# Clustered attention and a feed forward on one core: the first unit's transposed probabilities by halves in other banks, most weights made up later, the product with v by query tile, and other counts of places

## The chip, the cores and the metric

One core of one Trainium2 chip runs the kernel in one launch. The metric is the device time of an execution in microseconds (us). Before the change three runs gave a median of 846.21 us (845.62 to 848.19).

## The reference, cut to what matters

Attention over 4 batches, 8 heads, 768 positions and 64 columns a head, with a mask that lets a query see only the keys of its own cluster; the result, as 3072 tokens of 512 columns, goes through a feed forward of width 2048.

```python
def _attn_ref(q, k, v, centroids):
    ...
    q_assign = np.argmax(np.einsum('bhsd,hcd->bhsc', q_n, c_n), axis=-1)
    k_assign = np.argmax(np.einsum('bhsd,hcd->bhsc', k_n, c_n), axis=-1)
    mask = q_assign[:, :, :, None] == k_assign[:, :, None, :]
    scores = scale * np.matmul(q, k.transpose(0, 1, 3, 2))
    scores = np.where(mask, scores, -1000000000.0)
    scores = scores - np.max(scores, axis=-1, keepdims=True)
    attn = np.exp(scores)
    attn = attn / (np.sum(attn, axis=-1, keepdims=True) + 1e-09)
    return np.matmul(attn, v).astype(np.float32)

def _moe_ref(x, w_in, w_out):
    h = x @ w_in
    neg = h <= -1
    pos = h >= 1
    g = np.where(pos, h, np.where(neg, 0.0, (h + 1) ** 2 / 4))
    return (g @ w_out).astype(np.float32)
```

The weights arrive in float64; the kernel reads them as pairs of 32-bit words.

## The kernel before, in words

The work is cut into 12 units: a batch (4) and a third of its queries (256, in two query tiles t of 128). In a unit four head pairs hp follow each other, and in a pair four score tiles, one for each head j of the pair and query tile t. A score tile is 128 queries by 768 keys. TensorE writes it into a pair of banks (`pair`, two of them), VectorE adds the mask term and takes the row bound in one pass of 768 columns (`soften`, L1088, "score pass" below; it writes `sS`), and ScalarE takes the exponential with the row's sum (`at_soft`, L1104). The probabilities must then be transposed for the product with v.

In the first unit (`by_tensor`, L1138) all of this is in float32. TensorE transposes the tile in six matmuls of 128 columns into the same pair of banks that held the scores, and ScalarE copies 768 columns from there into `pT`. In all later units the tile is split into two float16 parts: ScalarE rounds it (`hl`), GpSimd subtracts the rounded part in two halves, and a DMA transpose issued on SP's queue brings both parts into `pT`. SP issues in its program's order.

The product with v (`at_av`, L1184) is a group of 72 matmuls of 64 columns for a head pair, both query tiles and both heads, in the first half of bank `banka`; VectorE scales it into `rb`, TensorE turns it back in the second half of that bank, and the result is `X[u]`, the feed forward's input.

The feed forward of a unit has eight columns f of 256. `ffn1` (L1347) multiplies X with `w_in` into one of three banks (`bankh`, `banki`, `bankj`, the ring `hid`); VectorE, ScalarE and VectorE again make the activation in `r`; ScalarE rounds it to `g`, GpSimd makes the remainder; `ffn2` multiplies with `w_out` into the second pair. The first unit's feed forward is float32 (`ffn1_first`, L1314), the later ones use float16 in two parts.

There are 16 blocks of weights, two for each f. A block is loaded in two halves (`w_load`, L1231), and `w_bits` (L1251) makes float32 from its word pairs: ScalarE takes the absolute value (1024 columns) into `wk`, VectorE shifts it (one TENSOR_SCALAR of 1024 columns) and combines twice (SCALAR_TENSOR_TENSOR of 1024 columns), and `w_sum` (L1279) has TensorE add columns up with a matrix of ones in 8 matmuls, of which VectorE takes a maximum (`w_am`). `w_split` (L1305) later makes the float16 parts.

The order is not written out by hand. Functions are filed under steps (`at`), the recorder notes every operation with a price and what it reads and writes, and a planner (`issue`, L363) sorts all engines' instructions by priorities: `BASE` passes forward and backward, then a table of numbers (`NUDGES`), each of which shifts the priorities of some functions. What is filed at a later step begins with a later priority. Buffers are rings (`new`, L546): the nth use of a ring of m places waits for the end of use n-m. The list `wat` holds the step of each block's `w_bits`. Before the change it runs from -4 by 2.2 a block. All recorded operations have the line L377 in the profile, so its rows are told apart by the names of their tiles.

Of the kernel before, what the change touches and what calls it, by code (L numbers as in the profile page):

```python
# [10 lines left out]
F16 = mybir.dt.float16  # L11
# [37 lines left out]
BASE = 3  # L49
NUDGES = (  # L50
# [422 lines left out]
class Ring:  # L473
# [4 lines left out]

    def __call__(self, *shape, dtype):
        self.i += 1  # L480
        return view(self.bufs[self.i % len(self.bufs)], shape, dtype)
# [16 lines left out]
def tile_clustered_attention_moe(  # L498
# [17 lines left out]
    P = 128  # L516
# [17 lines left out]
    WA, WR = -4, 2.2  # L534
# [34 lines left out]
    rings["x"] = Ring(tiles("x", 3, 4096) + wk[:1] + blocks[-1:] + [word[:, :1024], word[:, 1024:]])  # L569
# [17 lines left out]
    hid = Ring(one)  # L587
    start = cycle([0, 1]).__next__
# [96 lines left out]
    def batch_scale(b):  # L685

        e = BX[b]
        ar = misc(NP + 1)
# [82 lines left out]
    def k_first(hp):  # L771
# [12 lines left out]
        pn = misc(2, D)  # L784
# [60 lines left out]
    def k_scale(b, hp):  # L845
# [14 lines left out]
        ar = misc(1)  # L860
# [243 lines left out]
    def at_soft(b, hp, c, j, t):  # L1104
# [5 lines left out]
        if ("pT", j) not in e:  # L1110
            shape, kind = ([T, CT, P], F32) if by_tensor(b, c) else ([2 * T, CT, P], F16)
            e["pT", j] = new("pT", shape, kind, 3)
# [234 lines left out]
    def ffn1(u, f):  # L1347
        if u == 0:
            return ffn1_first(f)
        e = FS[u, f]  # L1350
        x = X[u]
        ph = hid(2, CQ, dtype=F32)
        for s in range(2):
# [204 lines left out]
```

## Time and profile before

| what | value |
|---|---|
| median of 3 runs | 846.21 us |
| the profiled execution | 844.95 us |
| its span, first to last instruction | 843.2 us |
| TensorE (PE) busy, with its granted clock over the span | 821.7 us, 0.992 |
| VectorE (DVE) busy | 633.7 us |
| ScalarE (ACT) busy | 645.7 us |
| GpSimd (POOL) busy | 481.3 us |
| DMA queue of SP, share of 16 rings' span | 83.2% |

The profile is of one execution. An engine's share is a mean over a start, in which keys, queries and weights are made ready and the first unit's attention runs, and a long stage, in which attention of later units and the feed forward of earlier ones share the engines; the rows by stretch tell the two apart. PE's busy time counts a matmul as long as it is modelled to be in the array, so a busy PE may still run at the lower clock, which the granted clock shows. DMA is the mean busy share of the 16 rings. A row of the timeline has its start, its length, and in brackets the idle time of its engine before it and what ended that.

### The profile page before, as it was taken

The numbers are of one execution on the slowest core, as the hardware profiler recorded it, in microseconds if no ns is written. First come the engines' busy times: TensorE is split into PE (matmuls) and PEld (weight loads), VectorE is DVE, ScalarE is ACT, GpSimd is POOL, SyncE is SP. The second block draws the span as 40 slices with busy tenths as digits, with TensorE's granted clock in tenths as the row PEclk, the third lists the DMA queues.
The fourth block names the chain that finished last, engine by engine and source line by source line (L and its number), as shares of the span: only waits on it lengthen the run. The fifth ranks groups of instructions, "written<-read, shape, count | busy, mean of one in ns | idle before, by whom it ended". The sixth has DMA issues, their size and how long they took to land.

```text
span 843.2 us, 21816 instructions
## 1 busy us (share of the span) xinstructions
PE 821.7 (97%) x8495; PEld 590.3 (70%) x8495; DVE 633.7 (75%) x1430; ACT 645.7 (77%) x1152; POOL 481.3 (57%) x541
## 2 busy tenths in 40 slices
PE   8887999999999999999999999999999999999998
PEld 6665667767666767776776777676676777777776
DVE  5899999989998787577897757678888767464322
ACT  5898978799977888888778788888787687675232
POOL 2012555466767768557667657667666577565122
PEclk9999999999999999999999999999999999999999
DMA  9866999989999989999999978999999887575000
GB/s 321 307 169 142 251 204 172 206 152 188 196 170 168 177 146 185 203 182 186 180 185 190 164 132 170 195 173 194 175 205 163 147 162 132 101 153 100 15 26 26
DMA packets 405415, 141.44 MB, mean 168 GB/s; under 512 B 373952, under 2 KB 397504, under 8 KB 405312
## 3 DMA queue, kind: packets, MB, share of 16 engines
q1 hardware_dynamic: 405312, 140.05, 83.2%
q8 instruction: 66, 1.08, 0.6%
q14 instruction: 37, 0.30, 0.1%
HBM read 40.40 MB, written 6.29 MB: 55 GB/s over the span
## 4 chain that ended last, share of the span: by engine, by line
PE 65%; DMA 2%; ACT 1%; issue 0%; DVE 0%; POOL 0%; ACTq 0%
PE pair L377 32%; PE banka L377 9%; PE banki L377 8%; PE bankh L377 8%; PE bankj L377 7%; DMA q<-qn 1%; DMA pT<-hl 1%; DMA kv<-n 1%; ACT sS L377 0%; POOL hl L377 0%; ACT hl L377 0%; ACT qn L377 0%; ACT q L377 0%; DVE sS L377 0%; DVE banki L377 0%
## 5 line engine op out<-in xcount | busy, mean ns | idle before, releaser
L377 POOL TENSOR_TENSOR hl<-sS,hl 128x384 f16<-128x384 f32 x352 | 334.5, 974 | 136.5 <-ACT hl L377 98.0
L377 PE MATMUL pair<-w,g 128*128 128x512 f16 (+2 forms) x1120 | 278.3, 387 | 0.0
L377 DVE CUSTOM_DVE_ANT_0 sS<-pair,zero,er 128x768 f32<-128x768 f32 x192 | 193.8, 1011 | 54.2 <-PE pair L377 36.1
L377 ACT ACTIVATE sS<-sS,sbi 128x768 f32<-128x768 f32 x192 | 179.0, 933 | 59.7 <-DVE sbi L377 52.3
L377 PEld LDWEIGHTS <-w 128*128 128x128 f16 x1848 | 179.2, 98 | 34.9 <-issue 1.5
L377 PEld LDWEIGHTS <-g 128*128 128x128 f16 x1104 | 105.9, 98 | 99.2
L377 PE MATMUL pair<-kv,q 128*128 128x384 f16 (+1 forms) x768 | 160.8, 345 | 2.1 <-ACT pT L377 0.7
L377 ACT CAST hl<-sS 128x768 f16<-128x768 f32 x176 | 144.2, 825 | 11.6 <-DMA pT<-hl 10.3
L377 POOL TENSOR_TENSOR g<-r,g 128x512 f16<-128x512 f32 x80 | 95.3, 1191 | 88.3 <-ACT g L377 79.4
L377 PEld LDWEIGHTS <-q 128*128 128x128 f16 x880 | 71.8, 98 | 45.3 <-issue 6.1
L377 PEld LDWEIGHTS <-pT 128*128 128x128 f16 x3168 | 98.3, 98 | 5.5 <-issue 1.1
L377 PE MATMUL banka<-kv,pT 128*128 128x64 f16 x3168 | 99.6, 193 | 0.0
L377 ACT ACTIVATE r<-r,f_ra,f_rs 128x512 f32<-128x512 f32 x80 | 64.8, 810 | 37.2 <-DVE r L377 36.8
L377 ACT CAST g<-r 128x512 f16<-128x512 f32 x80 | 48.8, 610 | 9.3 <-DVE r L377 6.4
L377 PE MATMUL bankj<-x,w 128*128 128x256 f16 (+1 forms) x368 | 47.9, 282 | 0.2 <-DVE r L377 0.2
L377 PE MATMUL bankh<-x,w 128*128 128x256 f16 (+1 forms) x320 | 42.0, 283 | 0.0
L377 PE MATMUL banki<-x,w 128*128 128x256 f16 (+1 forms) x280 | 41.5, 297 | 0.0
L377 POOL TENSOR_TENSOR qn<-qn,phi 128x256 f16<-128x256 f16 x44 | 26.7, 629 | 21.2 <-DVE bankj L377 5.3
L377 ACT ACTIVATION_READ_ACCUMULATOR sS<-sS,sbi 128x1 f32 x192 | 36.0, 187 | 0.0
L377 DVE TENSOR_SCALAR r<-bankh,f_lo,f_hi 128x512 f32<-128x512 f32 x27 | 21.8, 807 | 16.7 <-PE bankh L377 10.3
L377 DVE TENSOR_SCALAR r<-bankj,f_lo,f_hi 128x512 f32<-128x512 f32 x26 | 21.0, 806 | 16.6 <-PE bankj L377 10.5
L377 POOL CAST rr<-rs 128x4 f16<-128x4 f32 x4 | 2.8, 691 | 53.6 <-DVE bankh L377 29.2
(283 smaller groups left out, 1164.4 us busy)
## 6 DMA issues: line engine op xcount, KB each, us to landing
w<-in_moe_w_out_dram SPq DMA_DIRECT2D x14, 512.0 KB, 5.2
kv<-in_k_dram SPq DMA_DIRECT2D x16, 384.0 KB, 4.0
q<-in_q_dram SPq DMA_DIRECT2D x12, 512.0 KB, 4.8
kv<-in_v_dram SPq DMA_DIRECT2D x16, 384.0 KB, 5.1
out_dram<-o SPq DMA_DIRECT2D x11, 512.0 KB, 3.6
w<-in_moe_w_in_dram SPq DMA_DIRECT2D x10, 512.0 KB, 7.9
word<-in_moe_w_in_dram SPq DMA_DIRECT2D x6, 512.0 KB, 5.5
o<-in_v_dram SPq DMA_DIRECT2D x8, 384.0 KB, 3.9
```

The source lines that it names most:

```text
L377: fn(*args, **kw)
```

## The change

- In the first unit the transposes go, three at a time, into banks of the feed forward's ring `hid`, and each half of 384 columns is copied by itself. The pair of banks is no longer written by them.
- The step of the first 4 blocks' `w_bits` stays; those of the other 12 go to 14, 16, ... instead of 4.8, 7.0, .... The steps of the loads that reuse a place, of `w_scale` and `w_split` and of the first unit's feed forward follow from that list.
- Later units take their score tiles in the order of query tiles (both heads of t = 0, then of t = 1), `pT` is kept by query tile, and the product with v is two groups of 36 matmuls, one for each query tile. Product and turning back share one half of `banka`; the halves alternate (ring `av`).
- Small results (sums of weights, of squares, of ones) take a half of `banka` instead of a bank of `hid`.
- The ring of X has 3 places instead of 7. When the feed forward of unit 2 begins, the four places that were given up, with their sizes cut, extend the rings r, g, sS, hl and qn by one place each.
- `BASE` is 11 instead of 3, and the table of numbers is another one.

```diff
--- before.py
+++ after.py
@@ -46,38 +46,24 @@
 TURN, TURN_WAIT = dict(vector=185, gpsimd=118), 200
 
 LOOK, MARGIN = 0.4, 4000
-BASE = 3
+BASE = 11
 NUDGES = (
...
 )
 
 
@@ -476,6 +462,11 @@
     def __init__(self, bufs):
         self.bufs, self.i = bufs, -1
 
+    def extend(self, buf):
+
+        n = (self.i + 1) % len(self.bufs)
+        self.bufs, self.i = [buf] + self.bufs[n:] + self.bufs[:n], -1
+
     def __call__(self, *shape, dtype):
         self.i += 1
         return view(self.bufs[self.i % len(self.bufs)], shape, dtype)
@@ -531,7 +522,7 @@
     PRO = -14
     FA = SC + LA
     EARLY = 22
-    WA, WR = -4, 2.2
+    WA, WR, W2 = -4, 2.2, 14
     V_LATE, WG = 12.0, 2
 
     RAW = [3, 4, 5, 6, 7, 4, 5, 6, 0, 7, 6, 7, 0, 7, 0, 0]
@@ -566,7 +557,7 @@
     blocks = [wb[:, i * 1024 : (i + 1) * 1024] for i in range(2 * NF)]
     halves = wk[1:] + blocks[:-1]
     rings["w32"] = Ring(wk[:1])
-    rings["x"] = Ring(tiles("x", 3, 4096) + wk[:1] + blocks[-1:] + [word[:, :1024], word[:, 1024:]])
+    rings["x"] = Ring(tiles("x", 3, 4096))
     rings["g"] = Ring(tiles("g", 2, 2048))
 
     nb = tiles("n", 1, 2 * 3072)[0]
@@ -585,6 +576,7 @@
     pair = [psum.tile([P, 1024], F32, name=f"pair{i}") for i in range(2)]
     bank_a, *one = [psum.tile([P, 512], F32, name=f"bank{x}") for x in "ahij"]
     hid = Ring(one)
+    av = Ring([bank_a[:, :CQ], bank_a[:, CQ:]])
     start = cycle([0, 1]).__next__
 
     def early():
@@ -685,7 +677,7 @@
     def batch_scale(b):
 
         e = BX[b]
-        ar = misc(NP + 1)
+        ar = av(NP + 1, dtype=F32)
         am = e["am"].bitcast(BF16).rearrange("p (n a) -> p n a", a=2)[:, :, 1]
         rec.tensor.matmul(ar[:, :NP], ones, am, start=True, stop=True)
         mx = ar[:, NP:]
@@ -781,7 +773,7 @@
         )
         e["oneT"] = new("koT", [T * P], BF16)
         turned_ones(e["oneT"], one, T)
-        pn = misc(2, D)
+        pn = av(2, D, dtype=F32)
         with rec.group():
             for t in range(T):
                 rec.tensor.matmul(pn, ones, one[:, t], start=(t == 0), stop=(t == T - 1))
@@ -857,7 +849,7 @@
         rec.scalar.activation(out=junk, in_=e["k"].rearrange("p j f -> p (j f)"), func=AF.Square, accum_out=am)
 
 
-        ar = misc(1)
+        ar = av(1, dtype=F32)
         rec.tensor.matmul(ar, ones, am.bitcast(BF16)[:, 1:2], start=True, stop=True)
         sc = e["sc"] = new("sc", [1], F32, 2)
 
@@ -1107,24 +1099,26 @@
         sS, bi, pS = A.pop((b, hp, c, j, t))
         if "rs" not in e:
             e["rs"] = new("rs", [4], F32, 6)
-        if ("pT", j) not in e:
-            shape, kind = ([T, CT, P], F32) if by_tensor(b, c) else ([2 * T, CT, P], F16)
-            e["pT", j] = new("pT", shape, kind, 3)
+        m, w = (j, t) if by_tensor(b, c) else (t, j)
+        if ("pT", m) not in e:
+            shape, kind = ([T, CT, P], F32) if by_tensor(b, c) else ([2 * T, 2, P], F16)
+            e["pT", m] = new("pT", shape, kind, 3)
         sf = sS.rearrange("p a s -> p (a s)")
         rec.scalar.activation(
             out=sf, in_=sf, func=AF.Exp, bias=bi, scale=-1.0, accum_out=e["rs"][:, n : n + 1]
         )
-        pT = e["pT", j]
+        pT = e["pT", m]
         if by_tensor(b, c):
-            with rec.group():
-                for i in range(T):
-                    to = pS[:, i // 3, i % 3 * P : (i % 3 + 1) * P]
-                    rec.tensor.matmul(
-                        to, sf[:, i * P : (i + 1) * P], idf, start=(i % 3 == 0), stop=False, is_transpose=True,
-                        skip_group_check=True,
-                    )
-            pt = pS[:, :, :HS].rearrange("p h (n q) -> p h n q", q=P)
-            rec.scalar.copy(pT[:, :, t, :].rearrange("p (h n) q -> p h n q", h=2), pt)
+            for h in range(2):
+                ps = misc(T // 2, P)
+                with rec.group():
+                    for i in range(T // 2):
+                        x = (h * T // 2 + i) * P
+                        rec.tensor.matmul(
+                            ps[:, i], sf[:, x : x + P], idf, start=(i == 0), stop=(i == T // 2 - 1), is_transpose=True,
+                            skip_group_check=True,
+                        )
+                rec.scalar.copy(pT[:, h * T // 2 : (h + 1) * T // 2, t, :], ps)
             at_sums(e, n, b + c)
             return
         hl = new("hl", [2, S], F16, 3)
@@ -1132,7 +1126,7 @@
         for h in range(2):
             x = slice(h * HS, (h + 1) * HS)
             rec.gpsimd.tensor_tensor(out=hl[:, 1, x], in0=sf[:, x], in1=hl[:, 0, x], op=ALU.subtract)
-        rec.sync.dma_start_transpose(out=pT[:, :, t, :], in_=hl.rearrange("p a s -> p (a s)"))
+        rec.sync.dma_start_transpose(out=pT[:, :, w, :], in_=hl.rearrange("p a s -> p (a s)"))
         at_sums(e, n, b + c)
 
     def by_tensor(b, c):
@@ -1186,15 +1180,15 @@
         if u == 0:
             return at_av_first(hp)
         e, kv = A.pop((b, hp, c)), KV[b, hp]
-        pv, px = bank_a[:, :CQ], bank_a[:, CQ:]
-        with rec.group():
-            for t in range(CT):
+        pv = px = av(CQ, dtype=F32)
+        for t in range(CT):
+            with rec.group():
                 for j in range(2):
                     to = pv[:, (t * 2 + j) * D : (t * 2 + j + 1) * D]
                     for kc in range(T):
                         for i, (va, pa) in enumerate(((0, 0), (1, 0), (0, 1))):
                             rec.tensor.matmul(
-                                to, e["pT", j][:, pa * T + kc, t], kv["vs"][:, va, j, kc * D : (kc + 1) * D],
+                                to, e["pT", t][:, pa * T + kc, j], kv["vs"][:, va, j, kc * D : (kc + 1) * D],
                                 start=(kc == i == 0), stop=(kc == T - 1 and i == 2),
                             )
         xn = new("rb", [CT * 2, D], F32)
@@ -1282,7 +1276,7 @@
         n = 1024 if part is None else 512
         t = WL[a, f][:, (part or 0) * 512 :][:, :n]
         ab = t.bitcast(BF16).rearrange("p (f a) -> p f a", a=2)[:, :, 1]
-        pc = misc(P)
+        pc = av(P, dtype=F32)
         with rec.group():
             for x in range(n // P):
                 rec.tensor.matmul(pc, ones, ab[:, x * P : (x + 1) * P], start=(x == 0), stop=(x == n // P - 1))
@@ -1347,6 +1341,10 @@
     def ffn1(u, f):
         if u == 0:
             return ffn1_first(f)
+        if u == 2 and f == 0:
+            more = dict(r=wk[0][:, :512], g=wk[0][:, 512:], sS=word[:, :768], hl=word[:, 768:1536], qn=blocks[-1])
+            for name, buf in more.items():
+                rings[name].extend(buf)
         e = FS[u, f]
         x = X[u]
         ph = hid(2, CQ, dtype=F32)
@@ -1445,7 +1443,7 @@
     def at(step, fn, *args):
         ev.setdefault(step, []).append((fn, args))
 
-    wat = [WA + WR * i for i in range(2 * NF)]
+    wat = [WA + WR * i if i < 2 * WG else W2 + 2.0 * (i - 2 * WG) for i in range(2 * NF)]
     sf = 0
 
     def first(b, hp, c):
@@ -1485,7 +1483,7 @@
             for hp in range(NP):
                 s0 = first(b, hp, c)
                 for n in range(SC):
-                    j, t = divmod(n, CT) if u else (n % 2, n // 2)
+                    j, t = n % 2, n // 2
                     at(s0 + n, at_scores, b, hp, c, j, t)
                     at(s0 + n + 1, at_soft, b, hp, c, j, t)
                 at(s0 + (LA - 0.5 if u else LA - 1.5), at_av, b, hp, c)
```

On TensorE, the first unit, second query block of head pair 0 (`kv_62` holds head pair 1; `idf` is the identity). Before:

```order
L377 MATMUL pair_82<-idf,kv_64 64x128 x12
L377 MATMUL pair_83<-idf,sS_89 128x128 x6
L377 MATMUL bankj<-cf,kv_64 128x32 x6
L377 MATMUL pair_82<-idf,sS_88 128x128 x6
L377 LDWEIGHTS ones
L377 MATMUL banki<-wk_69,ones 128x128
...
L377 MATMUL pair_82<-kv_62,q_65 128x384
L377 MATMUL pair_83<-kv_62,q_65 128x384
L377 LDWEIGHTS hl_80
L377 MATMUL pair_82<-o_68,hl_80 128x384
```

After:

```order
L363 MATMUL bankj<-idf,sS_90 128x128 x3
L363 MATMUL pair_82<-kv_62,q_65 128x384
L363 MATMUL pair_83<-kv_62,q_65 128x384
L363 LDWEIGHTS hl_80
L363 MATMUL pair_82<-o_68,hl_80 128x384
...
L363 MATMUL bankj<-cf,kv_64 128x32 x6
L363 MATMUL banki<-idf,sS_88 128x128 x3
L363 LDWEIGHTS ones
L363 MATMUL banka<-wk_69,ones 128x128
...
L363 MATMUL banki<-idf,sS_89 128x128 x3
```

The transposes of a score tile stood between two uses of its pair of banks; now the next tile's scores are in the pair ahead of them, and the halves go into `banki`, `bankj` and `bankh`. The sum of a weights' block (`wk_69,ones`) has moved from `banki` to `banka`.

On VectorE, the first unit, from the 9th score pass (`ISA sS_88,sbi_135`) on; `wk_69` and `word_71` carry weights' words, `w_72` is the weights' memory. Before:

```order
L377 ISA sS_88,sbi_135<-pair_82,zero,er_132 128x768
L377 ISA sbi_135 128x1
L377 ISA sS_89,sbi_136<-pair_83,zero,er_132 128x768
L377 ISA sbi_136 128x1
L377 TENSOR_SCALAR wk_69<-wk_69 128x1024
L377 TENSOR_SCALAR banki<-banki 128x1
L377 SCALAR_TENSOR_TENSOR w_72<-w_72 128x1024
L377 TENSOR_SCALAR isx_165<-banki 128x1
L377 TENSOR_REDUCE w_am<-bankh 128x1
L377 TENSOR_REDUCE aq_160<-q_65 128x4
L377 SCALAR_TENSOR_TENSOR w_72<-w_72,wk_69 128x1024
L377 RECIPROCAL sv_168<-isx_165 128x1
```

After:

```order
L363 ISA sS_88,sbi_135<-pair_82,zero,er_132 128x768
L363 ISA sbi_135 128x1
L363 ISA sS_89,sbi_136<-pair_83,zero,er_132 128x768
L363 ISA sbi_136 128x1
L363 TENSOR_SCALAR banki<-banki 128x4
L363 TENSOR_SCALAR iq_161<-banki 128x4
L363 RECIPROCAL sq_163<-iq_161 128x4
L363 SCALAR_TENSOR_TENSOR n_78<-kv_61,sc_157,n_78 128x12x64
L363 SCALAR_TENSOR_TENSOR qn_67<-q_66,sq_163,qn_67 128x4x64 x4
L363 SCALAR_TENSOR_TENSOR w_72<-w_72 128x1024
L363 TENSOR_TENSOR x_73<-banka,rb_159 128x256
L363 SCALAR_TENSOR_TENSOR n_78<-kv_62,sc_158,n_78 128x12x64
```

Between the 9th pass and the 12 rows' end a shift, two combines and a maximum of weights (`wk_69`, `w_72`, `w_am`) stood in the queue; now one combine, and the remainders of k and q (`n_78`, `qn_67`) in their place.

## Rows read from the trace of the kernel before

**Rows 1.** Page, part 1: TensorE's busy time, share of the span, instructions.

```profile
PE 821.7 (97%) x8495; PEld 590.3 (70%) x8495; DVE 633.7 (75%) x1430; ACT 645.7 (77%) x1152; POOL 481.3 (57%) x541
```

**Rows 2.** Busy us by stretch: PE, PEld, DVE, ACT, POOL; clock, DMA share, GB/s.

```profile
24.00:83.56 59.56, 49.06 (x418) 36.43 (x419) 57.07 (x132) 54.22 (x95) 8.67 (x12) 0.91 0.71 198
83.56:190.65 107.09, 105.50 (x893) 73.95 (x893) 97.93 (x201) 90.56 (x160) 59.96 (x62) 0.98 0.96 197
190.65:262.18 71.53, 70.23 (x812) 49.91 (x811) 66.81 (x162) 61.17 (x106) 48.54 (x48) 1.00 0.99 178
85.51:839.32 753.81, 751.45 (x7853) 537.63 (x7853) 560.49 (x1257) 575.71 (x1037) 466.82 (x496) 1.00 0.85 160
```

**Rows 3.** Timeline of TensorE, two transposes of the first unit: start, length, [idle before].

```profile
68.22 2.27 PE L377 MATMUL pair<-idf,sS 128*128 128x128 f32 x12 [2.37 <-ACT sS L377]
...
85.51 2.31 PE L377 MATMUL pair<-idf,sS 128*128 128x128 f32 x12 [1.19 <-ACT sS L377]
```

**Rows 4.** Timeline of TensorE, the last matmuls.

```profile
838.50 0.82 PE L377 MATMUL banka<-w,g 128*128 128x256 f16 x6
```

**Rows 5.** Timeline of VectorE: the 11th, 16th and 60th score pass.

```profile
66.09 1.01 DVE L377 CUSTOM_DVE_ANT_0 sS<-pair,zero,er 128x768 f32<-128x768 f32 x1
...
83.56 1.01 DVE L377 CUSTOM_DVE_ANT_0 sS<-pair,zero,er 128x768 f32<-128x768 f32 x1
...
262.18 1.00 DVE L377 CUSTOM_DVE_ANT_0 sS<-pair,zero,er 128x768 f32<-128x768 f32 x1
```

**Rows 6.** Timeline of VectorE without a gap: a combine, two score passes, a maximum.

```profile
30.87 1.22 DVE L377 SCALAR_TENSOR_TENSOR w<-w,wk 128x1024 uint32<-128x1024 uint32 x1
32.00 1.01 DVE L377 CUSTOM_DVE_ANT_0 sS<-pair,zero,er 128x768 f32<-128x768 f32 x1
...
32.94 1.01 DVE L377 CUSTOM_DVE_ANT_0 sS<-pair,zero,er 128x768 f32<-128x768 f32 x1
...
35.11 0.28 DVE L377 TENSOR_REDUCE w_am<-bankj 128x1 f32<-128x128 f32 x1
```

**Rows 7.** VectorE by form, 24 to 96 us: busy us, mean ns | idle before.

```profile
L377 DVE SCALAR_TENSOR_TENSOR w<-w,wk 128x1024 uint32<-128x1024 uint32 x10 | 12.3, 1226 | 0.0
...
L377 DVE TENSOR_SCALAR wk<-wk 128x1024 uint32<-128x1024 uint32 x10 | 7.3, 731 | 0.4 <-ACT wk L377 0.4
```

**Rows 8.** Timeline of ScalarE in the first unit: copies, absolute value, 16th exponential's end.

```profile
44.58 0.35 ACT L377 COPY rb<-banka 128x256 f32<-128x256 f32 x1
...
46.21 1.15 ACT L377 ACTIVATE wk<-w 128x1024 f32<-128x1024 f32 x1
47.24 0.81 ACT L377 COPY pT<-pair 128x768 f32<-128x768 f32 x1
...
70.00 1.47 ACT L377 COPY pT<-pair 128x768 f32<-128x768 f32 x2
...
86.17 0.19 ACT L377 ACTIVATION_READ_ACCUMULATOR sS<-sS,sbi 128x1 f32 x1
```

**Rows 9.** VectorE by form, 96 to 160 us.

```profile
L377 DVE SCALAR_TENSOR_TENSOR w<-word 128x1024 uint32<-128x1024 uint32 x3 | 4.5, 1493 | 0.0
...
L377 DVE SCALAR_TENSOR_TENSOR w<-w 128x1024 uint32<-128x1024 uint32 x3 | 3.7, 1237 | 0.0
```

**Rows 10.** Busy time of a stretch of plain loads, and DMA issues of the page.

```profile
20.00:24.00 4.00, 2.86 (x36) 2.63 (x32) 3.90 (x13) 2.42 (x2) 0.00 (x0) 1.00 1.04 391
w<-in_moe_w_out_dram SPq DMA_DIRECT2D x14, 512.0 KB, 5.2
kv<-in_v_dram SPq DMA_DIRECT2D x16, 384.0 KB, 5.1
```

**Rows 11.** Timelines of VectorE and GpSimd: two long combines, and a subtraction beside them.

```profile
122.87 1.75 DVE L377 SCALAR_TENSOR_TENSOR word<-word,wk 128x1024 uint32<-128x1024 uint32 x1
...
124.88 1.84 DVE L377 SCALAR_TENSOR_TENSOR w<-word 128x1024 uint32<-128x1024 uint32 x1
...
124.72 2.77 POOL L377 TENSOR_TENSOR hl<-sS,hl 128x384 f16<-128x384 f32 x2 [1.18 <-ACT hl L377]
```

46 rows, old and new, of the table NUDGES are left out of this document.

## The prediction

> **What bounds the kernel now.** I read the page's engine shares first, then busy time by stretch, then the timeline of one engine at a time. The page gives TensorE 97% of the span [rows 1]; that is a mean over two stages. By stretch [rows 2] TensorE is busy 751.45 of the 753.81 us from 85.51 to 839.32, so from there on only 2.36 us can be won by any order. Before that the limit is VectorE: 57.07 of 59.56 us in the stretch from 24 to 83.56, in which the first unit's score passes lie, while TensorE works at a granted 0.91 and waits for ScalarE's exponentials (2.37 and 1.19 us [rows 3]). The last matmul ends at 839.32 [rows 4], and the output's way out takes the 3.9 us to the span's end. So the time is about 85.5 + 753.8 + 3.9 us inside the span: the change pays if TensorE becomes full earlier and then stays full. I count score passes (VectorE's 768-column pass over a pair of banks): the first unit's last is the 16th, at 83.56 [rows 5]; the 60th, at 262.18, is where the order has long made up all weights.
>
> **Term 1, VectorE up to the 16th pass.** Counted in the two instruction orders, the rows for weights that stand ahead of the 16th pass fall from 11 to 5 (shift, 1024 columns), from 19 to 10 (combine) and from 9 to 4 (maximum). A row ends about 0.08 us after the next can start (30.87 to 32.00 for a row of 1.22; 0.94 from pass to pass [rows 6]), so a shift costs 0.65, a combine 1.15 [rows 7], a maximum 0.20 [rows 6]. That takes away 6 x 0.65 + 9 x 1.15 + 5 x 0.20 = 15.2 us. One remainder of k and one of a weight now stand ahead instead, about 1.05 each: +2.1. Net 13 us: by VectorE alone the 16th pass could come at 70.5.
>
> **Term 2, ScalarE up to there.** Absolute values of weights ahead of the 16th exponential fall from 11 to 6, at 1.03 from start to start (46.21 to 47.24 [rows 8]): -5.2. The copies of turned probabilities go from 14 of 768 columns to 26 of 384. A copy of 768 takes 0.80, one of 256 takes 0.35 [rows 8]; one of 384 lies between them, on the line at 0.46, of which 0.1 overlaps the next. So 26 x 0.37 = 9.6 against 14 x 0.70 = 9.8: nothing (if 384 cost as much as 768, +8.4). Smaller rows moved behind: -1.2. ScalarE's 16th exponential ended at 86.36 [rows 8], 2.8 after its pass began, and would end 6.6 earlier: the pass at 77.0. But ScalarE is idle 5.3 of the 59.56 us [rows 2], since a pair of banks is held from its score pass (66.09 [rows 5]) through exponential and transposes (68.22 [rows 3]) until the copies of 70.00 are through [rows 8], 5.4 us. With the halves in other banks a pair is free after the pass itself. Without that idle time the pass comes at 71.6. I take 75, between 71.6 and 77: **8.5 us gained** so far.
>
> **Term 3, what was put off comes back.** From the 16th to the 60th pass three resources need nearly the whole stretch of 178.62 us. VectorE is busy 97.93 + 66.81 = 164.74 [rows 2]. To that come back the 13 us, and a surcharge: ahead of 96 us, with GpSimd nearly idle, a combine takes 1.22; from 96 to 160 it takes 1.24 to 1.49 [rows 7, 9], about 0.18 more, for nine of them 1.6 us. Three remainders of q, some 0.5 each, now stand behind the 60th: -1.5. That is 177.8. TensorE is busy 105.50 + 70.23 = 175.7, and gets about 5 us more (five blocks' sums and part of a column of the feed forward; by order, priced row by row): 180.7. The DMA rings are busy 0.96 and 0.99 of it, 173.6; in SP's order six half loads of weights (512 KB) and two of v (384 KB) that stood ahead of the first DMA transpose of probabilities now stand among the first 44, 3.8 MB at the 391 GB/s of a stretch of plain loads [rows 10] or 9.8 us, less one transpose of about 2: 181.4. Each load also stands ahead of transposes on SP, which issues in order, and TensorE's products wait for those. With the 16th pass at 75 the three alone would put the 60th at 252.8, 255.7 and 256.4. They cannot all run without a gap: VectorE left 4% idle even where it was the limit [rows 2]. I take 184 us, 1.5% above the largest: 259.0, **3.2 us earlier** than 262.18. The ends are 180.7 and 188 (4% above).
>
> **Term 4, the rest.** Behind the 60th pass the work is the same. The product with v is split by query tile: in the order 36 of 44 products now stand as two runs of 36 matmuls with other work between, 8 stay whole; the number of matmuls is the same, so the split costs nothing while TensorE is full. The second place for r, qn and the extra ones for g, sS and hl can win only what TensorE idles, 2.36 us; I take 0.5, between 0 and 2.4. X falls from 7 places to 3: in the new order the feed forward of unit 0 is through near the 38th pass, and X's fourth user writes near the 52nd, so nothing waits there. The small sums moved from the feed forward's banks into the product's bank cost the same.
>
> Sum: 3.2 + 0.5 = 3.7 us. The profiled execution took 844.95 us (span 843.2 and 1.75 around it), 1.26 under the median of 846.21. So 846.2 - 3.7 = **842.5 us**. A measurement of this kernel tells 0.3%, 2.5 us, from no change: under 843.7 is faster, over 848.7 slower.
>
> **Rivals.** *All given back.* If the stretch to the 60th pass takes 187 us, the lead of 8.5 is gone, and only term 4 is left: 845.7. For it: three full resources in one stretch, with the added loads among the transposes. Against it: before, VectorE had 13.9 us idle there, which the postponed rows can fill. Under this also falls that the halves don't free ScalarE (pass at 77) or that the new places are never needed.
>
> *Everything meshes.* The 16th pass at 71.6, the stretch in 180.7, and all of term 4: 9.9 + 2.3, about 834. For it: VectorE ran without a gap for 50 us in the old order. Against it: TensorE would have to be full from the 16th pass on.
>
> *Slower, by GpSimd.* Now 22 combines instead of 13 stand behind the 16th pass, where GpSimd subtracts the rounded probabilities all the time. Two such rows took 1.75 and 1.84 us when they met a subtraction, and the subtraction itself was longer [rows 11]. If all 22 paid 0.40 more on the path, 8.8 us are added: 851. From 0.28 each on the kernel is slower by the bound above (6.2 us over 22). Against it: other combines in the same stretch take 1.24 [rows 9]. The Trainium skill (SBUF — State Buffer, section SBUF: two separate sides) says that VectorE with two SBUF inputs and a GpSimd operation that reads SBUF exclude each other for the whole instruction. By that rule, the long rows agree: an estimate with half of a subtraction lost on each would be 853.
>
> **Chances and range.** Forecast 0.40, everything meshes 0.14, all given back 0.32, slower 0.14. So faster 0.54, same 0.32, slower 0.14. The range goes from 835 (nearly all of the meshing case; ends 71.6 and 180.7) to 849.5 (the stretch at 188 with the pass at 77 gives 848.5, and part of the GpSimd case).
>
> **What would show it.** Right: the 16th pass near 75 instead of 83.56, the 60th near 259, TensorE's last wait of over a microsecond before 80, and a later stretch that is as full as before. Term 2 is wrong if the pass stays past 77 with ScalarE idle; term 3 if VectorE, SP or the transposes open gaps on TensorE between 90 and 260; the GpSimd case shows as combines of 1.6 us and more. Outside the range the forecast fails by a gap in the long stretch, which I hold for full.

## The result, and the profile after

The changed kernel takes a median of 837.42 us (836.36 to 839.2, four runs) against 847.2 us (845.62 to 848.56, four runs) for the kernel before beside it: ratio 0.989, 95% interval 0.9865 to 0.9915, so 9.8 us or 1.1% faster. The profiled executions took 836.59 us (span 834.8) and 844.95 us (span 843.2); the 8.4 us between these two are what the traces can explain.

Page of the changed kernel, part 1, against [rows 1]:

```profile
PE 819.3 (98%) x8495; PEld 586.2 (70%) x8495; DVE 631.6 (76%) x1430; ACT 646.8 (77%) x1168; POOL 485.1 (58%) x541
```

TensorE idles 834.8 - 819.3 = 15.5 us of the span instead of 21.5, and is busy 2.4 us less with the same 8495 matmuls. Busy time by stretch of the changed kernel (columns as in [rows 2]), cut at its own 16th, 44th and 60th score pass, then the long full stretch:

```profile
24.00:72.14 48.14, 43.41 (x379) 28.98 (x378) 46.86 (x120) 46.84 (x98) 5.36 (x12) 1.00 0.77 213
72.14:185.60 113.46, 108.86 (x964) 76.47 (x962) 111.03 (x220) 95.51 (x169) 66.12 (x61) 1.00 0.95 198
185.60:255.19 69.59, 69.12 (x788) 49.44 (x786) 68.53 (x160) 61.84 (x107) 50.50 (x49) 1.00 0.90 177
72.14:255.19 183.05, 177.98 (x1750) 125.91 (x1748) 179.56 (x379) 157.35 (x275) 116.62 (x109) 1.00 0.93 190
85.06:830.90 745.84, 743.32 (x7819) 533.02 (x7817) 559.23 (x1251) 572.32 (x1026) 467.00 (x489) 1.00 0.85 163
```

Timeline of VectorE, the 16th and 60th pass, against 83.56 and 262.18 in [rows 5]:

```profile
72.14 1.01 DVE L363 CUSTOM_DVE_ANT_0 sS<-pair,zero,er 128x768 f32<-128x768 f32 x1
...
255.19 1.01 DVE L363 CUSTOM_DVE_ANT_0 word<-pair,zero,er 128x768 f32<-128x768 f32 x1
```

Timeline of TensorE, its waits of over a microsecond after the 16th pass, and the last matmuls, against [rows 3, 4]:

```profile
73.77 0.55 PE L363 MATMUL bankj<-idf,sS 128*128 128x128 f32 x3 [1.41 <-ACT sS L363]
...
83.84 0.81 PE L363 MATMUL pair<-kv,q 128*128 128x384 f16 x4 [1.22 <-DVE sbi L363]
...
830.14 0.82 PE L363 MATMUL banka<-w,g 128*128 128x256 f16 x6
```

The 16th pass comes 11.4 us earlier, the 60th 7.0. TensorE accounts for all of the 8.4 us. Its idle time by stretch, before and after:

| stretch | before | after |
|---|---|---|
| up to 24 us | 3.45 | 1.55 |
| from there to the 16th pass | 10.50 | 4.73 |
| 16th to 60th pass | 2.90 | 5.07 |
| 60th pass to the end | 4.67 | 4.20 |

That is 6.0 us less; the 2.4 us less of busy time (granted clock 1.00 from 24 on, against 0.91 up to the 16th pass) are the rest. From 8 to 24 us TensorE has no idle time any more; these 1.9 us stand in no term of the prediction. The last wait of over a microsecond ends at 83.84 instead of 85.51 (from 83.84 to 85.06 there is no gap), and by then TensorE has done 819.26 - 743.32 - 1.22 = 74.7 us of work instead of 821.67 - 751.45 = 70.2. From 85.06 to the last matmul it idles 2.52 us, against 2.36 from 85.51 [rows 2].

### The profile page after: what moved, and what is told of

Its sections match the earlier page's. It is cut to its first block, busy times and chain, and to the rows that moved or that the text cites. A ratio compares the mean times of both kernels' runs of the same rounds, so it can differ in the third digit from the quotient of the medians.

```text
span 834.8 us, 21762 instructions
## 1 busy us (share of the span) xinstructions
PE 819.3 (98%) x8495; PEld 586.2 (70%) x8495; DVE 631.6 (76%) x1430; ACT 646.8 (77%) x1168; POOL 485.1 (58%) x541
## 4 chain that ended last, share of the span: by engine, by line
PE 76%; DVE 14%; DMA 4%; issue 3%; ACT 2%; POOL 1%; SPq 0%; DVEq 0%; POOLq 0%
PE pair L363 37%; PE banka L363 11%; PE banki L363 10%; PE bankh L363 9%; PE bankj L363 9%; DVE sS L363 4%; DVE w L363 3%; DMA q<-in_q_dram 1%; DMA w<-in_moe_w_out_dram 1%; DVE r L363 1%; DVE n L363 1%; DVE wk L363 1%; POOL hl L363 1%; DMA pT<-hl 1%; DMA kv<-n 1%
## 5 line engine op out<-in xcount | busy, mean ns | idle before, releaser
L363 POOL TENSOR_TENSOR hl<-sS,hl 128x384 f16<-128x384 f32 x212 | 210.0, 1011 | 96.1 <-ACT hl L363 70.1
L363 PE MATMUL pair<-w,g 128*128 128x512 f16 (+2 forms) x796 | 202.6, 393 | 0.0
L363 PEld LDWEIGHTS <-q 128*128 128x128 f16 x880 | 71.6, 97 | 48.3 <-issue 8.0
L363 ACT CAST hl<-sS 128x768 f16<-128x768 f32 x106 | 87.4, 825 | 1.7 <-DMA pT<-hl 0.7
L363 PE MATMUL banki<-x,w 128*128 128x256 f16 (+1 forms) x672 | 86.0, 280 | 0.0
L363 PE MATMUL bankh<-x,w 128*128 128x256 f16 (+1 forms) x672 | 85.8, 280 | 0.1
L363 PEld LDWEIGHTS <-wk 128*128 128x128 f16 x606 | 58.0, 98 | 34.8 <-issue 0.6
L363 POOL TENSOR_TENSOR hl<-word,hl 128x384 f16<-128x384 f32 x70 | 63.1, 921 | 31.3 <-ACT hl L363 20.4
L363 POOL TENSOR_TENSOR word<-sS,word 128x384 f16<-128x384 f32 x70 | 64.0, 932 | 24.8 <-ACT word L363 22.6
L363 PE MATMUL pair<-w,wk 128*128 128x512 f16 x324 | 76.3, 373 | 0.0
L363 POOL TENSOR_TENSOR g<-r,g 128x512 f16<-128x512 f32 x32 | 39.8, 1244 | 26.1 <-ACT g L363 26.1
```

Of the source, the lines that this page charges most:

```text
L363: fn(*args, **kw)
```

## The experiments

Theory A: the parts of the code bring the gain, the place for the halves first. B: the newly found order brings it, that is the table and the 11 passes. C: the later weights bring it alone. In nine runs the table of numbers is empty and the order planned anew, since a table found for one code says nothing for another. The first two keep the planner's number of passes of their kernel, 11 and 3; for the other seven it was chosen anew, among 3 to 16. These nine (times are medians; the 16th and 60th score pass are those of one profiled execution):

| kernel, no table | time | ratio to before, interval | 16th pass | 16th to 60th |
|---|---|---|---|---|
| all parts | 840.66 | 0.9924, 0.9898 to 0.9949 | 73.25 | 186.45 |
| no part | 855.72 | 1.0107, 1.0072 to 1.0141 | 84.46 | 184.18 |
| without halves | 850.37 | 1.0039, 1.0018 to 1.0060 | 82.56 | 182.06 |
| without late weights | 848.67 | 1.0037, 1.0012 to 1.0063 | 78.92 | 184.31 |
| small results in the ring | 850.93 | 1.0049, 1.0031 to 1.0068 | 72.10 | 189.45 |
| product whole | 845.55 | 0.9983, 0.9971 to 0.9994 | 70.17 | 196.45 |
| without new places | 843.55 | 0.9966, 0.9953 to 0.9980 | 72.78 | 193.30 |
| halves alone | 851.57 | 1.0065, 1.0039 to 1.0091 | 79.71 | 186.26 |
| late weights alone | 858.74 | 1.0141, 1.0099 to 1.0183 | 83.06 | 190.24 |

**Code or order.** The table is taken out of the changed kernel, and out of the kernel before.

```diff
-NUDGES = (1525064232, ...)
+NUDGES = ()
```

> The changed kernel with the table of numbers taken out (no priorities shifted by it), BASE 11 kept: the code's parts remain, the found order goes. Theory A (the parts of the code bring the gain: places for the halves first, the later weights second): most of the gain stays; the table is worth 3 to 5 us to the changed kernel as it is to the kernel before, so about 841, still some 8 under the kernel before without its table. Theory B (the new table and BASE bring the gain, the parts are about neutral): 845 to 849, level with the kernel before without its table.

> The kernel before with its table taken out, BASE 3 kept. Both theories expect it slower than with the table, by 3 to 5 us: 849 to 852. Theory A wants it some 8 us above the changed kernel without its table, theory B level with it (within 2.5 us).

Without tables the parts gain 855.7 - 840.7 = 15.1 us, so the new table does not bring the gain. The number of planner's passes, B's other half, still differs here, 11 against 3. Against it speak the runs below: with a number of their own, undoing one main part costs 8.0 or 9.7 us, and one part alone put into the kernel before, with 11 or 16 of them, gains 4.1 us or nothing. The table is worth 3.2 us to the changed kernel, as expected, and 8.7 to the kernel before (847.0 beside it), more than expected: it may already have made up for part of what the code lacked there.

In the two profiles (spans 838.9 and 852.4) TensorE idles 20.9 and 26.6 us and is busy 818.0 and 825.8, with the same 8495 matmuls, at a mean granted clock of 0.995 and 0.989. So more than half of the difference lies in its busy time; how much of that is the clock's, these two do not tell.

**Halves undone.**

```diff
-for h in range(2):
-    ps = misc(T // 2, P)
...
+for i in range(T):
+    to = pS[:, i // 3, i % 3 * P : (i % 3 + 1) * P]
...
+rec.scalar.copy(pT[:, :, t, :].rearrange("p (h n) q -> p h n q", h=2), pt)
```

> The changed kernel without a table, and the first unit's transposes again all six in the pair of banks with one copy of 768 columns; the planner orders it anew (8 passes, the best of 3 to 16 by its own measure; 11 for the changed kernel). Theory A: the pair is held through exponential, transposes and copy again, ScalarE idles again about 5 us before the 16th score pass, the pass comes 4 us later or more, TensorE's clock falls again; 845 to 851, that is 4 to 10 above the changed kernel without its table. Theory B: within 2.5 us of it. A third theory, C (the later weights bring the gain, by VectorE alone): within 2.5 us of it, 16th pass near 72.

Busy time by stretch, up to the 16th pass: all parts, then without halves.

```profile
24.00:73.25 49.25, 40.93 (x365) 27.47 (x361) 46.37 (x115) 45.75 (x96) 7.06 (x12) 0.97 0.75 208
```

```profile
24.00:82.56 58.56, 47.07 (x387) 32.62 (x387) 51.26 (x129) 53.67 (x99) 7.72 (x13) 0.94 0.72 193
```

The pass comes 9.3 us later and the time rises by 9.7. ScalarE idles 4.9 us of the stretch instead of 3.5, and VectorE, which has its weights put off, 7.3 instead of 2.9: neither is full. The time is theory A's, and C falls. The date of the pass overstates the waiting: ScalarE is also busy 7.9 us longer ahead of it, mostly with rows that make keys and queries ready, and TensorE idles only 4.0 us more up to the pass.

**Late weights undone.**

```diff
-wat = [WA + WR * i if i < 2 * WG else W2 + 2.0 * (i - 2 * WG) for i in range(2 * NF)]
+wat = [WA + WR * i for i in range(2 * NF)]
```

> The changed kernel without a table, and the weights' bits asked for at the old steps (2.2 apart from -4 on); ordered anew (6 passes). Theory A: 13 us of VectorE stand ahead of the 16th pass again, so the pass comes at 80 or later; part of that is made up behind it since less weight work is left there: 2 to 6 us above the changed kernel without its table. Theory B: within 2.5 us. Theory C: all the gain goes, 8 us or more above.

The time rises by 8.0 us, more than theory A allowed and about C's least, though of a gain of 15.1. The pass comes at 78.92, 5.7 us later, and the stretch to the 60th gets 2.1 us shorter: so much of the lead is given back when weights are put off. At the 60th pass 3.5 us are lost, of 6.7 between the two profiled executions. TensorE idles 26.4 us of the span instead of 20.9, and 3.9 of these 5.5 lie between the two passes: weights asked for early cost most behind the 16th pass, which theory A did not expect. Why is open.

**One part alone.** The two main parts, each put by itself into the kernel before.

> The kernel before (no table, ordered anew, 11 passes) with one part of the change: the first unit's transposes by halves in the feed forward's banks. The kernel before without its table took 855.7 us with its 16th pass at 84.46; VectorE was busy 58.52 of the 60.46 us from 24 on. Theory A (parts that need each other): VectorE still has all its weights ahead, so the pass comes only 2 us earlier, and the time falls by 2 to 5 us, to 851 to 854. Rival (halves are the whole gain): 16th pass near 74, time near 841 to 844.

> The kernel before (no table, ordered anew, 16 passes) with one part of the change: the later steps for the bits of 12 blocks of weights. Theory A: VectorE is unloaded, but the pair of banks is held as before, so the 16th pass comes at 80 to 83 and the weights stand behind it: no gain, 853 to 857. Rival (late weights bring a gain by themselves): 16th pass at 77 or earlier, 848 or less.

Busy time by stretch, up to the 16th pass: halves alone, then late weights alone.

```profile
24.00:79.71 55.71, 46.34 (x431) 31.80 (x431) 54.97 (x131) 52.41 (x107) 5.32 (x12) 0.97 0.69 197
```

```profile
24.00:83.06 59.06, 45.56 (x414) 31.75 (x414) 55.43 (x133) 53.41 (x93) 7.47 (x13) 1.00 0.71 187
```

With the halves alone VectorE is busy 54.97 of 55.71 us: it is the bound. The pass comes 4.8 us earlier, more than theory A's 2, and 4.1 us are gained (the intervals overlap a little). With the late weights alone nothing is gained, and the pass moves by 1.4 us. For the date of the pass the parts need each other: alone they move it by 4.8 and 1.4 us, both together by 12.4, in the next run. For the time they are not enough: that run has both, with the split product and the new places, and lacks only the move of the small results; it is 4.8 us under no part, not 15.1.

**Small results back in the ring.** These stand in the prediction as free.

```diff
-pc = av(P, dtype=F32)
+pc = misc(P)
```

The four other `av(...)` of small results go back in the same way.

> The changed kernel (no table, 840.7 us; ordered anew, 5 passes) with its small results (sums of weights, squares and ones) back in the three banks of the feed forward. The prediction held this part for free. Theory A (only the halves and the later weights count): within 2.5 us of 840.7, 16th pass near 73. Rival (the ring of three banks must be kept for the halves): each sum takes a turn of the ring, TensorE or ScalarE waits for a bank, 16th pass 3 us later or more and 845 or more.

Waits of TensorE from 73 to 265 us (total, times, longest): this run, then all parts without a table.

```profile
PE pair L346 <- DVE sbi L346: 2.3, 5, 0.9
PE bankh L346 <- DVE w_am L346: 1.8, 2, 1.0
PE banki L346 <- DVE w L346: 1.5, 2, 1.2
PE bankh L346 <- DVE r L346: 1.3, 1, 1.3
PE banki L346 <- DVE banki L346: 1.0, 1, 1.0
PE banki L346 <- DVE r L346: 0.9, 3, 0.5
PE bankj L346 <- DVE g L346: 0.9, 1, 0.9
```

```profile
PE pair L346 <- DVE sbi L346: 2.0, 3, 1.3
PE banka L346 <- DVE wk L346: 1.0, 1, 1.0
PE banki L346 <- ACT pT L346: 0.9, 1, 0.9
```

As costly to undo as the halves: 10.3 us, with the 16th pass as early as ever, so the rival has the time right and not the place. From the 16th to the 60th pass TensorE idles 12.2 us instead of 5.5. In the rows shown it waits 7.4 us for VectorE at the banks h, i and j, 9.1 with the smaller ones; the other kernel's list has 0.2 of that. Two of these waits, 1.8 us, are for the maximum (`w_am`) itself: a sum holds one of three banks until VectorE has taken it. That the others follow from the same is argued, not shown: VectorE has 184.39 us of work in those 189.45, and whoever takes the next bank stands behind it, but it is as full with all parts (182.35 of 186.45).

**Product whole, and places undone.**

```diff
-pv = px = av(CQ, dtype=F32)
-for t in range(CT):
-    with rec.group():
+pv, px = bank_a[:, :CQ], bank_a[:, CQ:]
+with rec.group():
+    for t in range(CT):
```

```diff
-rings["x"] = Ring(tiles("x", 3, 4096))
+rings["x"] = Ring(tiles("x", 3, 4096) + wk[:1] + blocks[-1:] + [word[:, :1024], word[:, 1024:]])
...
-        rings[name].extend(buf)
```

> The changed kernel (no table, 840.7 us; ordered anew, 16 passes) with the product with v as before: score tiles by heads, one group of 72 matmuls, product and turning back in the two halves of the bank. Theory A: the split is worth 0 to 2.5 us, all of it behind the 16th pass (TensorE's idle time from there to the 60th grows from 5.5 us); 840 to 843. Rival (the split is what keeps TensorE fed while the weights come back): the 16th pass as early, but the stretch to the 60th 4 us longer or more, 845 or more.

> The changed kernel without a table, ordered anew (11 passes), with seven places for X and none lent to r, g, sS, hl and qn. Without a table the changed kernel took 840.7 us; TensorE there is idle 4.5 of the 705 us from 85 to 790. Theory A: 840 to 843; this also shows how far a newly found order alone moves the time. Rival (the places are what closes TensorE's last gaps): 844 or more, TensorE idle 8 us or more from 85 to 790.

The whole product (with the old order of score tiles) costs 4.9 us, all of it behind the 16th pass, as the rival said; in its profiled execution, the slowest of ten, TensorE idles 196.45 - 185.87 = 10.6 us to the 60th. The places cost 2.9 us, between the two theories: the time is A's, the 8.8 us of idle TensorE from 85 to 790 (in the slowest of eleven) is the rival's. A newly found order alone may move as much, and no run shows how much it does: the places are not settled, and the product's 4.9 is not far above them.

**The same order, one place changed.** These two keep the changed kernel's table and its order, as near as the dependencies allow; the first puts the halves into the pair, the second the small results into the ring.

```diff
-ps = misc(T // 2, P)
+misc(T // 2, P)
+ps = pS[:, h, : HS].rearrange("p (n q) -> p n q", q=P)
```

> The changed kernel with its table, and its order kept as near as the dependencies allow (each engine's instructions stand as in the changed kernel unless a buffer forbids it): the transposes and copies by halves stay, but the six transposes go into the pair of banks that held the scores, so nothing but the place differs. Theory A (the place frees the pair, and so ScalarE): the next scores wait for exponential, transposes and copies again, the 16th pass comes at 77 to 84 instead of 72.14, ScalarE idles 4 us or more of the stretch from 24 on, and the time is 842 to 848 instead of 837.4. Rival (smaller copies, or the order found with them, bring it): 837 to 840, 16th pass within 2 us of 72.

> The changed kernel with its table, and its order kept as near as the dependencies allow: only the small results (sums of weights, squares, ones) lie in the three banks of the feed forward again. Ordered anew and without a table this cost 10 us, with the 16th pass as early as before and 12.2 us of idle TensorE in the stretch to the 60th. Theory A (a sum holds one of three banks until VectorE, which is behind with its work, has taken the maximum, and feed forward and transposes wait for a bank): 842 or more here too, TensorE idle 4 us more from the 16th to the 60th pass, its waits for the h, i and j banks on VectorE. Rival (the order found for that run was poor): 837 to 840.

They took 873.25 us (ratio 1.0311, 1.0295 to 1.0328) and 925.09 us (1.0921, 1.0902 to 1.0940), the first far past theory A's 848, the second at the far end of its "842 or more". Busy time and ScalarE's longest wait up to 100 us, of the first:

```profile
24.00:105.78 81.78, 61.04 (x386) 39.10 (x385) 50.96 (x123) 49.66 (x100) 5.94 (x13) 0.77 0.50 132
```

```profile
ACT sS L350 <- DVE sbi L350: 20.8, 6, 4.5
```

The direction is theory A's, the size is no price of a place: in an order made for free banks, scores come late, and every engine waits in turn (ScalarE 20.8 us for score passes; up to the 16th pass no engine is busy over 75%). A misplaced buffer must be planned anew before it is priced.

**The clock.** The kernel before, with matmuls added to idle times of TensorE.

```diff
 for x in self.order:
+    for _ in range(FILL.get(x.i, 0)):
+        self.nc.tensor.matmul(self.pad, self.ones, self.ones, start=True, stop=True)
```

> The kernel before with its table and order, and 152 more matmuls of 128 columns in five of TensorE's idle times (ahead of the rows at 25.09, 52.57, 68.22, 83.69 and 85.51; 24, 36, 40, 32 and 20 of them, into the idle half of the product's bank), which nothing reads. Four of these five idle times are followed by rows at the lower clock (12 transposes take 2.78, 2.82 and 2.27 us instead of 1.53). If the added work keeps the granted clock at 1.00, the run shows what the clock was worth. Theory A (the clock is a side effect: TensorE's busy time as a whole is only 2.4 us less in the changed kernel): 844 to 847, 16th pass at 82 or later. Rival (TensorE at half speed sits in the chain from exponential to copy, and the restored clock is a large part of the gain): 839 to 843, 16th pass at 78 to 81. If the clock falls all the same, the run tells nothing of this.

Timeline of TensorE in this run, rows that were at the lower clock before, and two blocks that were added (L378):

```profile
23.64 1.50 PE L378 MATMUL banka<-ones 128*128 128x128 bf16 x24
25.34 1.79 PE L380 MATMUL pair<-idf,sS 128*128 128x128 f32 x12 [0.19 <-ACT sS L380]
...
52.15 1.79 PE L380 MATMUL pair<-idf,sS 128*128 128x128 f32 x12
...
67.48 2.82 PE L380 MATMUL pair<-idf,sS 128*128 128x128 f32 x12 [2.64 <-ACT sS L380]
...
73.00 0.25 PE L380 MATMUL banka<-idu,rr 128*64 128x128 f16 x2
...
76.83 2.41 PE L378 MATMUL banka<-ones 128*128 128x128 bf16 x40
```

Busy time by stretch: the granted clock is 1.00 where the idle time was filled, and falls where it was not.

```profile
48.00:56.00 8.00, 7.08 (x80) 5.40 (x78) 8.00 (x18) 7.94 (x16) 0.90 (x2) 1.00 0.99 198
...
64.00:72.00 8.00, 5.36 (x34) 4.46 (x32) 8.00 (x24) 7.50 (x14) 0.41 (x1) 0.79 0.27 51
```

The run took 844.84 us (ratio 0.9978, 0.9968 to 0.9988), 1.7 less than the kernel before beside it: theory A's range, as is its 16th pass at 84.28. As a price of the clock it is a lower bound only. The block of 40 stood behind the idle time it was meant for, so that stretch at half speed stayed, and its 2.41 us delayed the transposes behind it (and, landing in the product's bank before it was read, replaced a head pair's product of the first unit). Ahead of that block the row at 74.03 came at 73.00, with rows around 20 us starting 0.24 later: 1.3 us for two of the four stretches. What all four are worth stays open. Two other records narrow it. With the late weights alone the clock was 1.00 from 24 us to the 16th pass, and the pass still came at 83.06: the clock alone does not bring it forward. And the kernel before was timed 56 times beside these runs: the seven executions with a mean granted clock of 0.988 took 848.8 us on average, the eleven with 0.994 took 845.9. Carried on in proportion from its usual 0.992 to 1.00, beyond the highest clock measured (0.996), that is an estimate of 3 to 4 us of the gain. It only shows that clock and time go together, and in one of the three sets of these runs they hardly do.

## Why the prediction was right, point by point

**The direction and the sum.** Forecast 842.5, range 835 to 849.5, measured 837.42: faster, within the range, 5 us better than the likeliest case and on the way to "everything meshes". Profile against profile the sum was 3.7, measured 8.4: less than half was forecast, and it was the wide range that held the number. Of the 4.7 us between, 2.9 are the 16th pass, 0.95 the stretch to the 60th, and 0.9 what lies behind it. One sign failed: TensorE's last wait of over a microsecond was to end before 80, and ended at 83.84.

**Terms 1 and 2: mechanism right, size short.** VectorE was to allow the 16th pass at 70.5 and ScalarE at 77.0, at 71.6 without idle time; I took 75. It came at 72.14: ScalarE is busy 46.84 of 48.14 us, so its idle time nearly went. The choice between the two ends was 2.9 us too cautious. Runs without halves (82.56) and without late weights (78.92) show that the date needs both. The price of the small copy held; form of ScalarE's copies in the changed kernel, 24 to 96 us (busy us, mean ns), with 0.46 estimated:

```profile
L363 ACT COPY pT<-banki 128x384 f32<-128x384 f32 x11 | 5.4, 487 | 0.0
```

The prediction read the granted 0.91 and gave it no term; the 2.4 us of busy time went with it. Whether part of the 2.9 us is the clock's is not shown.

**Term 3: right, by partly wrong rows.** Forecast 184 us from the 16th to the 60th pass, measured 183.05. VectorE was put at 177.8 and is busy 179.56; TensorE at 180.7, and it is 177.98; the rings at 181.4, and they are busy 0.93 x 183.05 = 170 us: the late loads did not make them a bound. That 184 came so near is partly luck: it was 1.5% above a demand of the rings that did not exist, while the largest demand, VectorE's, lay 3.5 us below the measured stretch. The low end of 180.7 also lay below the sum's own 181.4.

**Term 4: two steps failed.** "The small sums moved from the feed forward's banks into the product's bank cost the same" priced the instructions and left out how long a bank is held: kept in the ring they cost 10.3 us. "The split costs nothing" is incomplete: the whole product, ordered anew, costs 4.9. Both act in the stretch behind the 16th pass, where I had only asked whether the lead is lost. The 0.5 us of idle time that the term expected did come behind the 60th pass (4.20 us instead of 4.67), though from 85 on TensorE idles 2.52 us instead of 2.36; no run ties it to the new places. The other 0.9 us gained behind the 60th pass are less busy time for as many matmuls (6161 against 6159); why is not shown.

**Rivals.** "All given back" did not occur, but the kernel before with late weights alone shows it. "Slower, by GpSimd" had its mechanism and not its size. Combines of the changed kernel by form, 72 to 185 us:

```profile
L363 DVE SCALAR_TENSOR_TENSOR w<-w 128x1024 uint32<-128x1024 uint32 x7 | 10.3, 1475 | 0.0
L363 DVE SCALAR_TENSOR_TENSOR w<-w,wk 128x1024 uint32<-128x1024 uint32 x7 | 9.6, 1372 | 0.0
...
L363 DVE SCALAR_TENSOR_TENSOR word<-word,wk 128x1024 uint32<-128x1024 uint32 x4 | 5.9, 1478 | 0.0
L363 DVE SCALAR_TENSOR_TENSOR w<-word 128x1024 uint32<-128x1024 uint32 x4 | 5.3, 1320 | 0.0
```

The 22 take 31.1 us, 1.41 each, 0.19 above the 1.226 of [rows 7]; the sum had 0.18, the rival wanted 0.28 or more. The longest, and the subtraction beside it (two take 1.79 us at 99.93):

```profile
104.38 1.92 DVE L363 SCALAR_TENSOR_TENSOR w<-w 128x1024 uint32<-128x1024 uint32 x1
```

```profile
104.30 2.77 POOL L363 TENSOR_TENSOR hl<-sS,hl 128x384 f16<-128x384 f32 x2 [2.59 <-ACT hl L363]
```

Seven of the 22 take over 1.5 us, the others keep near 1.2 to 1.45. The Trainium skill (SBUF — State Buffer, section SBUF: two separate sides) says that of a VectorE operation with two SBUF inputs and a GpSimd operation that reads SBUF, the one that starts first keeps the shared ports to its end, and the other waits. The long rows agree with it; what failed is my estimate that every combine would meet a subtraction.

## What to carry to other kernels

Where several resources bound the same stretch, price parts together: here each of the two main parts alone gained 4.1 us or nothing, all but the move of the small results 4.8, and the whole 15.1. The date of a pass is a sign and no price: the pass came 12.4 us earlier for those 4.8. Count how long a small result holds a shared buffer until its reader gets to it, not only what its instructions cost. Before pricing a part of a kernel whose order was searched for, take the search out on both sides, or plan each version anew: the found table hid 8.7 us in one kernel and 3.2 in the other, and a frozen order turned a cost of 10 us into 36 and 88.

## What was not expected of the hardware

In the kernel before, TensorE's granted clock fell to 0.50, 1.2 GHz (as from 52.70 to 55.30), behind idle times of 1.53, 2.01 and 2.37 us, and behind two of 1.78 and 1.19 with 8 matmuls between them. Timeline of TensorE, the first:

```profile
25.09 2.78 PE L377 MATMUL pair<-idf,sS 128*128 128x128 f32 x12 [1.53 <-ACT sS L377]
```

The same 12 transposes took 1.79 us at 25.34 once the idle time ahead of them was filled. In the changed kernel no wait from 14 to 90 us is longer than 1.41, and the clock stayed at 1.00, 2.4 GHz, with no work added. But the length of one wait does not decide it. With the late weights alone the same 12 transposes took 1.79 us at the full clock behind waits of 2.94 and 2.62 us, and 2.82 us, at 0.50, behind one of 2.98:

```profile
26.24 1.79 PE L346 MATMUL pair<-idf,sS 128*128 128x128 f32 x12 [2.94 <-ACT sS L346]
...
67.29 1.79 PE L346 MATMUL pair<-idf,sS 128*128 128x128 f32 x12 [2.62 <-ACT sS L346]
...
84.39 2.82 PE L346 MATMUL pair<-idf,sS 128*128 128x128 f32 x12 [2.98 <-ACT sS L346]
```

What sets the two kinds apart, no run here shows.
